# One set of weights a slot, behind the transposes, in an attention and mixture-of-experts kernel, and a new table of step times

## The chip, the cores and the metric

The kernel runs on one core of a Trainium2 chip. The metric is the device time of one execution in microseconds (us). Before the change it is 494.95 us, the median of three runs (494.95 to 495.12).

## What is computed

A causal attention with a memory term, then a layer of eight experts of which each token uses one.

```python
scores = scale * np.matmul(q, k.transpose(0, 1, 3, 2))      # q, k, v: (4, 8, 576, 64)
a = softmax(where(causal, -1e9, scores)); local = a @ v
mem_out = (phi(q) @ M_prev) / (phi(q) . z_prev + 1e-6)
x = g * mem_out + (1 - g) * local                            # 2304 tokens of 512
expert_idx = np.argmax(x @ w_gate, axis=1)                   # 8 experts
for e in range(8):                                           # w1[e]: 512x1024, w2[e]: 1024x512, float32
    xe = x[expert_idx == e]
    out[mask] = gate_w[mask] * (np.maximum(xe @ w1[e], 0) @ w2[e])
```

## The kernel before

**Attention** (`attention`, to about 262 us of the span) is cut into some 545 steps. Each step has a time in units of one pair of heads: a base from the table `K` plus a shift from `K["sh"]`, and the steps are written out sorted by that time, which a scheduler then interleaves further. The table is thus the order of the work on every engine.

**The experts** (`experts`) are written by hand, engine by engine, with semaphores and with branches on the counts that the routing found. Work goes in *slots*: 128 tokens of one expert (a full slot) or 64 (a half one). With these inputs there are 23: expert 0 (in the kernel's own order) has slots 0 to 3, expert 1 slot 4, expert 2 slots 5 to 11, expert 3 slot 12 (half), expert 4 slots 13 to 18 (18 half), expert 5 slot 19 (half), expert 6 slots 20 and 21 (21 half), expert 7 slot 22 (half). Slot 0 is mostly done beside the end of attention. In each slot

- PE multiplies the tokens `xT` by w1 into `ph` (L1632, 96 matmuls), and then the relu of it by w2 into `m_py` (L1648, 24 matmuls; L1645 in half slots). Numbers are kept as a high and a low float16 part.
- DVE makes the two relu parts (L1812, L1814), copies the next slot's transposed tokens to `xT` (L1858), and splits the gathered tokens of the slot after that into `m_xn` (L1835, L1837).
- ACT takes `m_py` out (L1774); POOL gathers tokens for a later slot (L1532) and scatters results (L1547).
- SP issues the two DMA transposes of `m_xn` into `m_xB` (`xtrans`, L1443) and the loads of weights (`load`, L1414).

**Weights** of an expert are eight units of 512 KB, in two *sets* of four: set 0 and 1 are expert 1's, 2 and 3 expert 2's, to 13 for expert 7 (`half_of`). A set is loaded as float32 into one of two stages and converted one set a slot: ACT makes the high part (`conv_hi`, L1302), DVE the low part (`conv_lo`, L1306). In this run sets 0 to 7 are converted in slots 1 to 8, sets 8 to 11 in slots 13 to 16, sets 12 and 13 in slots 19 and 20. Set 0 is loaded during attention.

**SP's queue** in the experts is the place of the change. SP first waits for two gathers and loads set 1. Then each slot has a `turn` or a `rest`: `slot()` issues the transposes of the next slot's tokens as soon as DVE has copied this slot's and made the next `m_xn`, and then come the loads. `ld` counts the sets that were loaded. `turn(i)` belongs to the slot that converts set i, and loads set i+2 in the ordinary case; `rest` belongs to a slot without conversion, and loads each of two sets that is still due. Before L1414 a load waits until the stage that it writes was converted.

```python
for j in (2 * e + 4, 2 * e + 5):          # rest
    if j < 14:
        with SP.If(SP.snap(ld) < j + 1):
            load_next(j)
```

Of the kernel before, what the change touches and what calls it, by code (L numbers as in the profile page):

```python
# [17 lines left out]
K = dict(wa=(6, 0, 2, 0, 0, 1, 1, 1, 1, 1, 2, 0, 3, 0, 1, 1, 1, 1, 0, 0, 1, 0, 0), d=3.668, wt=4, wu=0, wv=0, w3=46, wl1=(17.6, 17.7, 17.9, 18.0), room=48,  # L18
         sz=(2.047, 2.265, 2.085, 2.03), cr=-2.149, cast1=-1.166, tk1=-0.422, phi0=0.086, pt0=1.165, x0=(19.233,
         19.268), e0=(19.944, 21.6), s0=(1.627, 2.769), s1=(0.965, 1.642), p0=(3.152, 2.79), n1=(-0.81, -1.106),  # L20
         n2=(0.194, 0.959), p1=(1.9, 3.343), wd=(8, 8), nc1=0, pact=11, wact=0, pact1=2, wact1=0, nc3=0, cuts=((1,
         2), (0, 0)), rc=7.911, r0=(15.971, 18.056), r1=(19.042, 22.191), ap=(17.127, 17.643), al=(17.821, 18.944),
         at=(19.653, 20.088), k1=-1.476, setup=1.937, v1=2.277, sw=(3.049, 3.089, 3.067, 3.374), sm=(3.763, 3.551,
         3.508), cast=-0.886, castd=0.017, tk=-0.427, tq=-0.544, phi=0.497, pt=2.14, lk=-1.909, lq=-1.882, lv=0.695,
         n=(-0.15, 0.75), s=(1.052, 2.002), p=(2.014, 3.031), m0=(4.286, 4.261), m7=(2.592, 3.428), m=(2.511, 3.7),
         a0=(4.4, 4.852), a=(3.988, 5.201), wl=(14.447, 14.146, 15.631, 16.029, 16.835, 17.187, 17.16, 17.947),
         wc=(15.676, 17.094, 15.773, 17.231, 17.473, 17.338, 18.21, 17.972), sh=dict(m_steps1w=0.45, wconv01=0.43,
         s_steps14w=0.24, a_steps4=1.03, const_q1=3.25, n_first68=0.2, first_q2=0.12, m_steps2w=0.27,
         p_steps2w=-0.01, wload03=-0.03, wconv03=-1.21, s_first12=0.4, setup=-1.59, n_steps4=-0.13, s_steps6w=-0.51,
         p_steps0=0.37, s_steps13=-0.07, phi21=1.15, wload06=1.12, s_steps8w=0.79, wload10=0.62, load6k=-0.45,  # L30
         setup_w0=0.03, n_steps15=-0.7, n_steps13=0.15, n_steps2w=-0.23, load5q=0.2, p_steps12w=0.65,
         bothtrans_piece1=-0.1, load6v=0.06, load2v=-0.16, load4q=0.08, wload13=1.53, wload01=1.01, s_steps12=0.17,
         load1k=-3.84, m_steps7w=-0.93, s_first01=0.72, load_pieceq0=-0.83, n_first56=0.08, p_steps1w=-0.29,
         m_steps5w=0.14, load0v=0.44, n_steps11=-0.23, wload05=-0.16, n_steps12w=-0.49, s_steps3=0.18,
         wconv00=-0.14, a_steps6w=-0.57, p_steps8w=-0.28, n_steps11w=-0.18, cast_q50=-0.25, p_steps9w=-0.37,
         wconv02=-0.38, load5k=-0.19, wconv06=0.84, phi40=0.24, n_first89=0.06, phi60=-0.06, cast_q71=-0.03,
         setup_m2=0.42, cast_k01=0.07, phi50=-0.54, a_steps7=-0.19, cast_q20=-0.12, n_steps7=-0.24, m_steps4=0.95,
         p_steps4=-0.02, p_steps13w=0.12, trans7QT1=0.19, s_first37=0.59, load3k=0.47, m_steps3=0.39,
         s_steps10w=-0.31, wload04=0.19, cast_k10=-0.58, load0k1=0.23, setup_m1=0.24, setup_w3=-0.1, p_steps13=0.3,
         s_steps8=-0.02, setup_w2=0.11, a_steps0w=-0.32, phi70=-0.08, setup_z1=0.65, s_steps9=-0.09, trans0PT=0.42,  # L40
         p_steps14=0.54, p_steps5=0.26, setup_z0=0.25, phi10=-0.14, trans2PT=0.17, p_steps0w=-1.61, cast_k11=0.6,
# [1213 lines left out]
def experts(nc, tc, es, x_dram, mem, rout, w1, w2, out):  # L1255
# [29 lines left out]
    with tc.tile_critical():  # L1285
# [159 lines left out]
        def loads(j):  # L1445

            if j < 14:
                for e, u in half_of(j):
                    if e > 2 and split(e - 2, u) > 0:
                        SP.wait_ge(S["clo"], 16 + split(e - 2, u))  # L1450
                    load(e, u)

        SP.wait_ge(S["g0"], 16)
        SP.wait_ge(S["gg"], 16)
        for u in range(NL, 8):
            load(1, u)
# [3 lines left out]
        SP.reg_mov(ld, 2)  # L1460
# [4 lines left out]
        for e in range(NE):  # L1465
# [16 lines left out]
            def turn(i):  # L1482
                slot()
                if i == c0:
                    SP.wait_ge(S["sc0"], 16)
                    SP.sem_inc(S["ya"], 1)
                SP.reg_add(cr, cr, 1)
                with SP.If(SP.snap(ld) < i + 1):
                    load_next(i)
                with SP.If(SP.snap(ld) < i + 2):  # L1490
                    load_next(i + 1)
                with SP.Else():
                    with SP.If(SP.snap(ld) < i + 3):
                        load_next(i + 2)

            def rest():
                slot()
                for j in (2 * e + 4, 2 * e + 5):
                    if j < 14:
                        with SP.If(SP.snap(ld) < j + 1):  # L1500
                            load_next(j)
# [407 lines left out]
```

## Time and profile before

| | |
|---|---|
| median of three runs | 494.95 us |
| the profiled execution's own time | 495.53 us |
| its span, first to last instruction | 493.8 us |
| PE busy | 458.9 us, 93% |
| DVE, ACT, POOL busy | 355.1, 222.4, 219.5 us |
| attention, about | 0 to 262 us |
| experts, about | 262 to 493.8 us |

How to read it: an engine's busy time counts its own instructions. The chain of waits follows the last instruction back to what released it, again and again. "issue" in it is time in which an engine waited for nothing that the profile shows. The granted clock is 1.00 at TensorE's 2.4 GHz and 0.50 at 1.2 GHz.

### The profile page before, as it was taken

Reading aid. Unit: us, or ns where it says so; the run is one execution under the profiler, and the core shown is the slowest. Engines: PE = TensorE matmul, PEld = TensorE weight load, DVE = VectorE, ACT = ScalarE, POOL = GpSimd, SP = SyncE. Lnnn points to the kernel's source line nnn. Section 1 sums busy time; section 2 is a strip of 40 time slices with the busy share of each in tenths; the row PEclk is TensorE's granted clock in tenths of the full one; section 3 lists DMA queues with packets and bytes.
Section 4 is the critical chain, followed back from the end, with each engine's and each line's share of the span. In section 5 each row is a group of like instructions: output and inputs, shape, how many; then the busy total and the mean of one; then the engine's idle time right before and its main releaser. Section 6 shows DMA issues by size and latency. Waiting matters only on the chain.

```text
span 493.8 us, 14324 instructions
## 1 busy us (share of the span) xinstructions
PE 458.9 (93%) x5274; PEld 311.9 (63%) x5275; DVE 355.1 (72%) x785; ACT 222.4 (45%) x363; POOL 219.5 (44%) x397
## 2 busy tenths in 40 slices
PE   2999889999999989999998899899999998999995
PEld 0654456566566645656675577677667776777865
DVE  3898678687868746889876587788863458874694
ACT  3687665565566556365713324543300033430611
POOL 7467558367748235546542332322232322323332
PEclk9999899999999999999999989999999999999999
DMA  5567979899899979989442999979843393893522
GB/s 119 128 117 167 185 147 174 159 186 217 173 181 166 255 164 178 192 189 288 140 145 76 271 339 300 254 258 284 286 152 90 100 366 83 244 261 100 85 66 73
DMA packets 170184, 90.85 MB, mean 184 GB/s; under 512 B 151487, under 2 KB 152767, under 8 KB 170112
## 3 DMA queue, kind: packets, MB, share of 16 engines
q1 hardware_dynamic: 166192, 77.95, 67.2%
q0 software_dynamic: 3920, 12.10, 7.9%
q8 instruction: 26, 0.43, 0.4%
q14 instruction: 46, 0.38, 0.3%
HBM read 55.64 MB, written 11.60 MB: 136 GB/s over the span
## 4 chain that ended last, share of the span: by engine, by line
PE 61%; SPq 9%; DVE 9%; DMA 8%; issue 7%; ACT 3%; POOL 2%; POOLq 1%; DVEq 0%; ACTq 0%
PE ph L1632 17%; PE m_py L1648 15%; PE o L566 7%; PE st L492 5%; PE sm L597 3%; SPq L276 3%; DMA m_xB<-m_xn 2%; SPq L278 2%; DMA QT<-mem 2%; PE loc L678 2%; PE sn L405 2%; SPq L1443 1%; DVE mem L1306 1%; PE wm L883 1%; DMA mem<-in_q_dram 1%
## 5 line engine op out<-in xcount | busy, mean ns | idle before, releaser
L1632 PE MATMUL ph<-m_xT,mem 128*128 128x128 f16 (+1 forms) x1344 | 68.9, 214 | 5.1 <-DVE m_xT L1858 3.8
L1632 PEld LDWEIGHTS ph<-m_xT,mem 128*128 128x128 f16 x1344 | 67.4, 99 | 8.8 <-issue 6.9
L1812 DVE TENSOR_SCALAR m_hT<-ph 128x512 f16<-128x512 f32 (+1 forms) x44 | 27.7, 630 | 53.2 <-PE ph L1632 43.8
L1774 ACT ACTIVATE m_y<-m_py 128x512 f32<-128x512 f32 x17 | 10.2, 597 | 123.8 <-PE m_py L1648 84.2
L496 POOL TENSOR_SCALAR_AFFINE_SELECT aT<-aT 128x128 f32<-128x128 f32 (+2 forms) x160 | 48.8, 322 | 38.1 <-ACT aT L511 36.0
L511 ACT ACTIVATE aT<-st 128x512 f32<-128x512 f32 x96 | 54.8, 594 | 19.5 <-PE st L492 19.0
L413 DVE TENSOR_REDUCE mt<-sn 128x1 f32<-128x512 f32 (+4 forms) x83 | 54.2, 663 | 13.0 <-PE sn L411 10.4
L1648 PE MATMUL m_py<-mem,m_hT 128*128 128x512 f16 x264 | 58.9, 379 | 0.8 <-DVE m_hT L1812 0.8
L566 PE MATMUL o<-aT,mem 128*64 128x448 f32 (+4 forms) x320 | 57.9, 433 | 0.7 <-POOL aT L496 0.7
L1582 POOL COPY m_ig<-r_idx 128x1 int32 x22 | 12.1, 548 | 96.4 <-DVE m_xn L1835 95.2
L492 PE MATMUL st<-mem 128*128 128x64 f16 (+6 forms) x224 | 46.6, 259 | 0.7 <-ACT aT L511 0.3
L1648 PEld LDWEIGHTS m_py<-mem,m_hT 128*128 128x128 f16 x264 | 25.3, 98 | 29.3 <-DVE mem L1306 0.9
L1632 PE MATMUL ph<-m_xT,m_w 128*128 128x128 f16 (+1 forms) x768 | 42.0, 216 | 1.7 <-issue 1.7
L1632 PEld LDWEIGHTS ph<-m_xT,m_w 128*128 128x128 f16 x768 | 41.1, 98 | 3.8 <-issue 2.1
L492 PEld LDWEIGHTS <-mem 128*128 128x128 f16 (+1 forms) x448 | 32.8, 98 | 16.8 <-issue 5.3
L492 PE MATMUL st<-QT,mem 66*128 66x64 f16 (+6 forms) x224 | 41.7, 259 | 0.0
L1648 PE MATMUL m_py<-m_w,m_hT 128*128 128x512 f16 x168 | 37.4, 379 | 0.0
L1532 POOL DMA_INDIRECT m_xg<-x_scratch,m_ig x23 | 26.3, 1141 | 22.9 <-POOL m_ig L1582 15.8
L566 PEld LDWEIGHTS o<-aT,mem 128*64 128x64 f32 x320 | 22.8, 137 | 18.0 <-issue 11.2
L1547 POOL DMA_INDIRECT out_dram<-m_y,m_is x23 | 24.0, 1042 | 19.6 <-POOL m_is L1553 15.4
L405 PE MATMUL sn<-mem 128*128 128x128 f16 (+3 forms) x158 | 31.4, 276 | 0.5 <-DVE mt L413 0.2
L1814 DVE SCALAR_TENSOR_TENSOR m_hT<-ph,m_hT 128x512 f16<-128x512 f32 (+1 forms) x44 | 27.7, 630 | 1.5
(264 smaller groups left out, 911.0 us busy)
## 6 DMA issues: line engine op xcount, KB each, us to landing
mem<-in_moe_w_dram SPq DMA_DIRECT2D x40, 512.0 KB, 5.0
m_stage<-in_moe_w_dram SPq DMA_DIRECT2D x24, 512.0 KB, 6.9
mem<-in_k_dram SPq DMA_DIRECT2D x32, 128.0 KB, 2.9
mem<-in_q_dram SPq DMA_DIRECT2D x32, 128.0 KB, 3.0
mem<-in_v_dram SPq DMA_DIRECT2D x32, 128.0 KB, 2.8
x_scratch<-xb SPq DMA_DIRECT2D x3, 1152.0 KB, 5.8
mem<-mem SPq DMA_DIRECT2D x6, 288.0 KB, 3.8
x_scratch<-xb SPq DMA_DIRECT2D x1, 864.0 KB, 3.8
```

Source lines behind the costliest of these rows:

```text
L405: nc.tensor.matmul(ps[:, c:c + k1 - k0], QT[:, 5 * hh + t, :], keys(hh)[:, k0:k1], start=(c == 0), stop=(k1 == parts[-1][3] and hh == part ...
L413: nc.vector.reduce_max(out, v, axis=AX.X)
L492: nc.tensor.matmul(ps[:, c:c + n], kk[:, kb, :], qq[:, w:w + n], start=(first and i == 0 and j == 0), stop=(last and i == 1 and j == len(p ...
L496: nc.gpsimd.affine_select(out=ap, in_=ap, pattern=pattern, compare_op=ALU.is_ge, fill=0.0, base=base, channel_multiplier=-1)
L511: nc.scalar.activation(out=a, in_=ps, func=AF.Exp, scale=ESC)
L566: nc.tensor.matmul(o[64 * hh:64 * hh + 64, q0:q0 + n], vv, aa, start=(j == 0), stop=(j == 4), skip_group_check=True)
L1532: G.indirect_dma_start(out=x.rearrange("p h e -> p (h e)"), out_offset=None, in_=x_dram, in_offset=bass.IndirectOffsetOnAxis(ap=i, axis=0) ...
L1547: G.indirect_dma_start(out=out, out_offset=bass.IndirectOffsetOnAxis(ap=i, axis=0), in_=ysb[:, j], in_offset=None, bounds_check=bound, oob ...
L1632: mm = PE.matmul(ph[i2][:, f, 0:N], w[:, kc, c:c + 128], x[:, j, kc, 0:N], start=(i == 0), stop=(i == 11), skip_group_check=True)
L1648: mm = PE.matmul(py, hh, ww[:, 4 + ff // 2, c:c + 512], start=st, stop=sp_)
L1812: V.tensor_scalar(out=hT[i2][0][:, :, 0:N], in0=ph[i2][:, :, 0:N], scalar1=0.0, scalar2=None, op0=ALU.max).then_inc(S[hi], 1)
L1814: V.scalar_tensor_tensor(out=hT[i2][1][:, :, 0:N], in0=ph[i2][:, :, 0:N], scalar=0.0, in1=hT[i2][0][:, :, 0:N], op0=ALU.max, op1=ALU.subtr ...
```

## The change

Two things. The table `K` has other numbers for many of the steps, some of which then stand at another place; two of its lines before and after (`d`: a shift of all the sums of the softmax, `wl1`: the loads of set 0, `p_steps0`: the first product of scores and v):

```diff
-K = dict(wa=(6, 0, 2, 0, 0, 1, 1, 1, 1, 1, 2, 0, 3, 0, 1, 1, 1, 1, 0, 0, 1, 0, 0), d=3.668, wt=4, wu=0, wv=0, w3=46, wl1=(17.6, 17.7, 17.9, 18.0), room=48,
...
-         p_steps0=0.37, s_steps13=-0.07, phi21=1.15, wload06=1.12, s_steps8w=0.79, wload10=0.62, load6k=-0.45,
+K = dict(wa=(6, 0, 2, 0, 0, 1, 1, 1, 1, 1, 2, 0, 3, 0, 1, 1, 1, 1, 0, 0, 1, 0, 0), d=3.629, wt=4, wu=0, wv=0, w3=46,
...
+         s_first12=0.62, setup=-1.73, n_steps4=-0.11, s_steps6w=-0.55, p_steps0=-0.69, s_steps13=-0.07, phi21=0.72,
```

And SP's loads: set 1 is no longer loaded ahead of the first transposes; every turn loads at most one set, the first that is due; the wait for the first scatter (`sc0`) stands behind the loads.

```diff
             if j < 14:
                 for e, u in half_of(j):
+                    if e == 1 and u < NL:
+                        continue
                     if e > 2 and split(e - 2, u) > 0:
                         SP.wait_ge(S["clo"], 16 + split(e - 2, u))
                     load(e, u)
-        SP.wait_ge(S["g0"], 16)
-        SP.wait_ge(S["gg"], 16)
-        for u in range(NL, 8):
-            load(1, u)
...
-        SP.reg_mov(ld, 2)
+        SP.reg_mov(ld, 1 + NL // 8)
...
-            def turn(i):
+            def first_of(js):
+                if js and js[0] < 14:
+                    with SP.If(SP.snap(ld) < js[0] + 1):
+                        load_next(js[0])
+                    with SP.Else():
+                        first_of(js[1:])
+
+            def turn(i, both=False):
                 slot()
+                SP.reg_add(cr, cr, 1 + both)
+                first_of((i, i + 1, i + 2))
+                if both:
+                    first_of((i, i + 1))
                 if i == c0:
                     SP.wait_ge(S["sc0"], 16)
                     SP.sem_inc(S["ya"], 1)
-                SP.reg_add(cr, cr, 1)
-                with SP.If(SP.snap(ld) < i + 1):
-                    load_next(i)
-                with SP.If(SP.snap(ld) < i + 2):
-                    load_next(i + 1)
-                with SP.Else():
-                    with SP.If(SP.snap(ld) < i + 3):
-                        load_next(i + 2)
 
             def rest():
                 slot()
-                for j in (2 * e + 4, 2 * e + 5):
-                    if j < 14:
-                        with SP.If(SP.snap(ld) < j + 1):
-                            load_next(j)
+                first_of(tuple(range(2 * e + 2, 2 * e + 6)))
```

SP's instructions where the experts begin, before (`mem_61` is here the odd experts' stage, so the first DMA row is set 1; `m_stage` is the even experts' stage, `r_cnt` the counts of slots):

```order
L1905 UNCONDITIONAL_BRANCH
L1414 DMA mem_61<-in_moe_w_dram 128x2x512 x4
L1463 TENSOR_LOAD r_cnt
L1464 TENSOR_LOAD r_cnt
L1513 COMPARE_AND_BRANCH
L1515 COMPARE_AND_BRANCH
L1469 ISA
L1516 COMPARE_AND_BRANCH
L1438 ISA
L1443 DMA_TRANSPOSE m_xB<-m_xn_4177 128x4x128
L1442 REGISTER_ALU
L1443 DMA_TRANSPOSE m_xB<-m_xn_4178 128x4x128
```

The same place in the changed program, where load is L1415, the transpose L1444 and the ladder of branches L1483:

```order
L1515 COMPARE_AND_BRANCH
L1439 ISA
L1444 DMA_TRANSPOSE m_xB<-m_xn_4177 128x4x128
L1443 REGISTER_ALU
L1444 DMA_TRANSPOSE m_xB<-m_xn_4178 128x4x128
L1473 TENSOR_LOAD r_cnt
L1475 TENSOR_LOAD r_cnt
L1490 ISA
L1483 COMPARE_AND_BRANCH
L1483 UNCONDITIONAL_BRANCH
L1483 COMPARE_AND_BRANCH
L1415 DMA mem_61<-in_moe_w_dram 128x2x512 x4
```

The four loads of set 1 moved from ahead of the first two transposes to behind them.

SP's instructions in the `rest` of expert 3 (slot 12), before; each load row stands behind a branch of its own:

```order
L1443 DMA_TRANSPOSE m_xB<-m_xn_4178 128x4x128
L1474 TENSOR_LOAD r_cnt
L1476 TENSOR_LOAD r_cnt
L1500 COMPARE_AND_BRANCH
L1414 DMA m_stage_4185<-in_moe_w_dram 128x1024 x4
L1500 UNCONDITIONAL_BRANCH
L1500 COMPARE_AND_BRANCH
L1414 DMA m_stage_4185<-in_moe_w_dram 128x2x512 x4
```

And in the changed program; after each load a jump leads out of the ladder:

```order
L1473 TENSOR_LOAD r_cnt
L1475 TENSOR_LOAD r_cnt
L1483 COMPARE_AND_BRANCH
L1415 DMA mem_61<-in_moe_w_dram 128x1024 x4
L1483 UNCONDITIONAL_BRANCH
L1483 COMPARE_AND_BRANCH
L1415 DMA mem_61<-in_moe_w_dram 128x2x512 x4
L1483 UNCONDITIONAL_BRANCH
L1483 COMPARE_AND_BRANCH
L1415 DMA m_stage_4185<-in_moe_w_dram 128x1024 x4
L1483 UNCONDITIONAL_BRANCH
L1483 COMPARE_AND_BRANCH
```

Before, both sets (10 and 11) go out in this slot; now one of the four choices does, which is set 10, and set 11 is left to a later turn.

In attention, PE at the first product of scores and v (`p_steps0`, `o`), in the changed program:

```order
L884 MATMUL wm<-r_id_66 128x512
L556 MATMUL sl<-aL,mem_61 64x64 x2
L567 MATMUL o<-aT,mem_61 64x512 x2
L567 MATMUL o<-aT,mem_61 64x448 x2
L567 MATMUL o<-aT,mem_61 64x320 x2
L567 MATMUL o<-aT,mem_61 64x192 x2
L567 MATMUL o<-aT,mem_61 64x64 x2
L332 LDWEIGHTS mem_59
```

Before, these ten matmuls stood one or two at a time between transposes and scores of the next heads over some 150 rows; now they are one block ahead of those transposes.

## Rows read from the trace of the kernel before

**Rows 1.** The page: busy us, share of the span and instructions of each engine.

```profile
PE 458.9 (93%) x5274; PEld 311.9 (63%) x5275; DVE 355.1 (72%) x785; ACT 222.4 (45%) x363; POOL 219.5 (44%) x397
```

**Rows 2.** Chain of waits, slots 2 to 4: start us, us, what.

```profile
283.24 7.15 PE ph L1632 x96
290.39 5.18 PE m_py L1648 x24
295.57 5.36 PE ph L1632 x96
...
306.11 5.36 PE ph L1632 x96
```

**Rows 3.** Timeline, slot 1: start us, us, engine, line, what, count, [idle before].

```profile
270.44 0.48 DVE L1835 TENSOR_SCALAR m_xn<-m_xg 128x512 f16<-128x512 f32 x1
270.49 1.93 SPq L1414 DMA_DIRECT2D mem<-in_moe_w_dram  x4
...
274.23 3.19 SPq L1443 DMA_TRANSPOSE m_xB<-m_xn  x2
...
275.92 5.34 PE L1648 MATMUL m_py<-mem,m_hT 128*128 128x512 f16 x24
...
280.73 0.18 POOL L1553 COPY m_is<-r_ids 128x1 int32 x1 [5.66 <-SPq L1486]
...
282.67 0.43 DVE L1858 COPY m_xT<-m_xB 128x1024 f16<-128x1024 f16 x1 [4.00 <-DMA m_xB<-m_xn]
...
283.24 7.15 PE L1632 MATMUL ph<-m_xT,mem 128*128 128x128 f16 x96 [1.98 <-DVE m_xT L1858]
```

**Rows 4.** Windows: us; busy PE, PEld, DVE, ACT, POOL; granted clock; DMA share, GB/s.

```profile
55.00:58.50 3.50, 3.50 (x16) 1.25 (x16) 2.27 (x2) 2.84 (x3) 1.82 (x3) 0.52 0.96 176
...
283.80:287.20 3.40, 3.40 (x36) 3.40 (x34) 2.75 (x3) 2.29 (x3) 1.96 (x3) 0.50 1.02 354
```

**Rows 5.** Chain of waits, slots 12 to 14.

```profile
392.50 0.38 SPq L1414
...
398.42 3.39 SPq L1443
...
401.99 7.35 DMA m_xB<-m_xn
```

**Rows 6.** Timeline, slots 12 to 14.

```profile
397.20 0.75 DVE L1837 SCALAR_TENSOR_TENSOR m_xn<-m_xg,m_xn 128x512 f16<-128x512 f32 x1
...
402.84 5.34 PE L1648 MATMUL m_py<-mem,m_hT 128*128 128x512 f16 x24
...
410.00 4.18 PE L1632 MATMUL ph<-m_xT,mem 128*128 128x128 f16 x72 [1.82 <-DVE m_xT L1858]
```

**Rows 7.** Line 1414, the 52 loads of weights in the experts.

```profile
DMA to landing us min/median/max: 3.4/5.9/9.6
```

**Rows 8.** Timeline, slots 3 and 4: loads, and the next slot's conversion.

```profile
298.56 2.17 SPq L1414 DMA_DIRECT2D mem<-in_moe_w_dram  x4
...
307.97 3.90 ACT L1302 ACTIVATE m_w<-m_stage 128x1024 f16<-128x1024 f32 x4 [1.09 <-issue]
...
310.16 1.22 DVE L1306 SCALAR_TENSOR_TENSOR m_w<-m_stage,m_w 128x1024 f16<-128x1024 f32 x1
...
311.30 5.34 PE L1648 MATMUL m_py<-mem,m_hT 128*128 128x512 f16 x24
...
311.50 0.69 DVE L1812 TENSOR_SCALAR m_hT<-ph 128x512 f16<-128x512 f32 x1
```

**Rows 9.** Timeline, slots 20 and 21: transposes with no load ahead of them.

```profile
476.29 2.56 SPq L1443 DMA_TRANSPOSE m_xB<-m_xn  x2
...
481.87 0.43 DVE L1858 COPY m_xT<-m_xB 128x1024 f16<-128x1024 f16 x1 [1.03 <-DMA m_xB<-m_xn]
```

**Rows 10.** PE's waits in attention (0 to 262 us): us in total, times, longest.

```profile
PE mem L632 <- DMA mem<-mem: 2.6, 2, 2.1
PE st L531 <- DMA QT<-mem: 1.9, 4, 0.8
```

More of the change, by code (lines that the diff above doesn't have):

```diff
@@ new lines @@
+K = dict(wa=(6, 0, 2, 0, 0, 1, 1, 1, 1, 1, 2, 0, 3, 0, 1, 1, 1, 1, 0, 0, 1, 0, 0), d=3.629, wt=4, wu=0, wv=0, w3=46,
+         wl1=(17.749, 17.651, 17.759, 18.218), room=48, sz=(2.047, 2.258, 2.085, 2.03), cr=-2.438, cast1=-1.166,
+         tk1=-0.422, phi0=0.086, pt0=1.4, x0=(19.233, 19.268), e0=(19.954, 21.001), s0=(1.627, 2.769), s1=(0.934,
+         1.642), p0=(3.152, 2.829), n1=(-0.948, -1.042), n2=(0.155, 0.922), p1=(1.978, 3.343), wd=(8, 8), nc1=0,
+         pact=11, wact=0, pact1=2, wact1=0, nc3=0, cuts=((1, 2), (0, 0)), rc=7.839, r0=(15.971, 18.056), r1=(19.042,
+         22.084), ap=(17.237, 17.643), al=(17.821, 19.616), at=(19.771, 20.088), k1=-1.454, setup=1.979, v1=2.357,
+         sw=(3.049, 3.089, 3.067, 3.374), sm=(3.763, 3.551, 3.469), cast=-0.886, castd=0.022, tk=-0.34, tq=-0.561,
+         phi=0.488, pt=2.261, lk=-1.909, lq=-1.889, lv=0.652, n=(-0.15, 0.75), s=(1.049, 2.002), p=(2.014, 3.019),
+         m0=(4.315, 4.261), m7=(2.592, 3.428), m=(2.511, 3.7), a0=(4.376, 4.858), a=(3.988, 5.201), wl=(14.447,
+         14.146, 15.631, 16.029, 16.835, 17.187, 17.16, 17.947), wc=(15.676, 17.037, 15.773, 17.231, 17.473, 17.96,
+         18.205, 18.15), sh=dict(m_steps1w=0.49, wconv01=-0.51, s_steps14w=0.14, a_steps4=1.03, const_q1=3.25,
+         n_first68=0.2, first_q2=0.12, m_steps2w=0.27, p_steps2w=-0.01, wload03=-0.03, wconv03=-1.21,
+         s_first12=0.62, setup=-1.73, n_steps4=-0.11, s_steps6w=-0.55, p_steps0=-0.69, s_steps13=-0.07, phi21=0.72,
+         wload06=1.83, s_steps8w=0.79, wload10=0.88, load6k=-0.45, n_steps15=-0.7, n_steps13=0.13, n_steps2w=-0.23,
+         load5q=0.2, p_steps12w=0.65, bothtrans_piece1=-0.1, load6v=0.06, load2v=-0.16, load4q=0.08, wload13=1.54,
+         wload01=1.01, s_steps12=0.16, load1k=-3.84, m_steps7w=-0.93, s_first01=0.72, load_pieceq0=-0.76,
+         n_first56=0.08, p_steps1w=-0.29, m_steps5w=0.14, load0v=0.44, n_steps11=-0.24, n_steps12w=-0.49,
+         s_steps3=0.18, wconv00=-0.18, a_steps6w=-0.57, p_steps8w=-0.36, n_steps11w=-0.18, cast_q50=-0.25,
+         p_steps9w=-0.39, wconv02=-0.38, load5k=-0.13, wconv06=1.47, phi40=0.24, n_first89=0.06, phi60=-0.06,
+         cast_q71=0.31, setup_m2=0.42, cast_k01=0.15, phi50=-0.54, a_steps7=-0.19, cast_q20=-0.52, n_steps7=-0.24,
+         m_steps4=0.95, p_steps4=-0.02, p_steps13w=0.12, trans7QT1=0.19, s_first37=0.59, load3k=0.47, m_steps3=0.39,
+         s_steps10w=-0.33, wload04=0.75, cast_k10=-0.58, load0k1=0.23, setup_m1=0.24, setup_w3=-0.1, p_steps13=0.22,
+         s_steps8=-0.07, setup_w2=0.11, a_steps0w=-0.32, phi70=0.21, setup_z1=0.59, s_steps9=-0.09, trans0PT=0.42,
+         p_steps14=0.54, p_steps5=0.26, setup_z0=0.33, phi10=-0.14, trans2PT=0.33, p_steps0w=-1.47, cast_k11=0.96,
+         p_steps9=-0.02, cast_q60=0.07, wload17=0.84, n_steps15w=0.38, a_steps3=0.2, p_steps6w=0.69, wconv05=0.66,
+         wconv04=0.27, m_steps7=-0.32, phi01=-0.03, trans4KT1=-0.22, a_steps2=-0.1, a_steps2w=-0.01, m_steps5=-0.02,
+         s_steps12w=-0.89, s_steps14=0.07, p_steps10=0.76, cast_q41=-0.29, trans5QT1=0.18, a_steps7w=-1.04,
+         s_steps7=-0.15, p_steps11w=-0.84, phi41=1.02, s_steps9w=0.16, p_steps8=0.87, bothcast_piece2=0.08,
+         n_steps5w=-0.15, p_steps5w=0.15, s_steps1=0.07, trans7PT=0.13, wconv10=1.48, m_steps4w=-0.84,
+         cast_k50=-0.01, p_steps6=0.12, phi30=-0.42, s_steps4w=0.16, s_steps11=-0.14, m_steps6w=-0.84,
+         n_first1011=0.52, p_steps10w=-0.55, cast_k71=-0.47, n_steps1w=0.4, p_steps7w=0.75, cast_k41=-0.1,
+         p_steps11=0.2, trans3PT=-0.58, d_steps5=-0.52, cast_k30=-0.12, load0q1=-0.61, n_steps10=0.22,
+         load_pieceq1=-0.09, n_steps6w=0.02, trans_pe11=0.41, setup_z3=0.19, d_steps2w=0.41, cast_q11=-0.49,
+         n_steps10w=-0.22, trans4QT1=-0.07, d_steps1=0.18, s_steps10=0.27, n_steps7w=-0.08, cast_k51=-1.06,
+         n_steps9w=-0.32, s_steps5w=-0.04, a_steps4w=0.05, wconv11=-0.74, s_steps5=0.04, d_steps4w=0.92,
+         p_steps15=0.01, routing1=0.4, routing1w=1.2, s_steps3w=-0.16, cast_k61=-0.31, phi20=0.58, s_steps6=0.47,
+         phi71=0.53, s_steps15w=-0.12, warm1=-0.03, bothcast_piece1=-0.09, d_steps0=0.3, setup_w1=0.03,
+         d_steps3=0.25, n_steps6=0.05, m_steps3w=0.09, load2q=-0.14, a_steps3w=0.24, wload11=0.87, cast_q10=-0.49,
+         warm2=1.9, setup_m0=-0.72, d_steps0w=-0.26, wload15=-0.67, routing0=0.05, n_steps5=-0.26,
+         bothcast_piece0=0.04, const_k1=-0.62, phi31=0.29, s_steps11w=0.12, warm3=2.56, cast_k40=-0.79,
+         d_steps7w=-0.42, cast_q31=-0.9, n_steps1=-0.59, wconv07=0.92, d_steps1w=0.17, n_steps9=-0.04, phi00=-0.02,
+         a_tail7w=-0.05, load_pieceq2=0.05, a_pre7w=1.29, wload00=0.6, trans_pe10=0.27, setup_z2=-0.38,
+         const_k0=-0.08, trans5PT=0.05, load_piecek2=0.12, bothtrans_piece0=0.05, n_first25=0.08, cast_q40=0.03,
+         n_steps4w=0.29, load1q=1.54, s_steps15=0.2, d_steps6w=-0.25, s_first23=0.34, d_steps4=-0.99, a_tail7=0.66,
+         trans2QT1=0.01, a_last7w=-1.53, bothtrans_piece2=0.02, n_steps12=0.41, cast_q21=0.16, early_x0=0.66,
+         load3v=-0.02, p_steps14w=0.37, a_pre7=-0.8, const_rest=-0.08, cast_k70=-0.67, a_steps1w=0.03, load7q=0.03,
+         a_last7=0.66, trans7KT1=-0.29, p_steps3w=0.22, d_steps5w=-0.11, trans5KT1=-0.2, a_steps6=0.01,
+         wload02=-0.5, early_x0w=-0.01, trans6KT1=0.23, n_first910=-0.11, cast_q30=-0.28, trans6PT=-0.04,
+         trans2KT1=-0.03, phi61=-0.22, load4k=-0.33, const_k2=-0.57, phi11=0.51, load_piecek1=-0.07, load4v=-0.02,
+         s_steps2=0.34, a_steps5w=0.03, cast_k31=-0.33, first_k2=0.5, cast_k21=0.34, p_steps4w=-0.06, fill46=0.76,
+         n_steps14w=0.02, a_steps1=0.56, trans3KT1=-0.39, cast_k20=0.44, wload07=0.98, p_steps1=0.13, p_steps7=0.04,
+         cast_q51=0.42, early_p0w=0.36, n_steps8w=0.01, s_steps13w=0.05, n_first02=0.03, n_steps14=-0.02,
+         d_steps3w=0.02, m_steps0=-0.11, s_steps4=-0.03, cast_q70=-0.05, n_steps8=0.04, d_steps2=-0.1, consts=-0.03,
+         p_steps15w=0.06, n_steps3w=0.1, trans6QT1=0.06, cast_q01=-0.08, load1v=-0.08, trans3QT1=0.06,
+         early_p0=-0.08))
@@ L1518, in experts @@
                             with SP.Else():
-                                turn(now[0])
-                                SP.reg_add(cr, cr, 1)
+                                turn(now[0], True)
                     with SP.If(SP.snap(cr) < 2 * e + 2):
```

52 lines of the change are left out of this document (removed).

## The prediction

> **What bounds the kernel now.** I read the page first: TensorE is busy for 93% of the span [rows 1], so time can only come from the places where it stands still or runs slowly. Then I went along the chain of waits through the experts, slot by slot. The reader is to see a steady beat there: a full slot is 5.36 us of `ph` and 5.18 us of `m_py`, and the next slot begins 306.11 - 295.57 = 10.54 us after the last [rows 2]. Almost every full slot keeps it. Two do not, and both lead back to SP's queue.
>
> *Stall A, before slot 2.* `m_py` of slot 1 starts at 275.92 [rows 3]. At the steady 5.18 us [rows 2] the next `ph` could start at 281.10; it starts at 283.24 [rows 2], 2.14 us late. The row names DVE's copy of the transposed tokens, which itself waited 4.00 us for the transposes' DMA [rows 3]. SP issued those transposes at 274.23, behind the four loads of set 1 (270.49), though DVE began to make their input at 270.44 [rows 3]. And slot 2's `ph` then takes 7.15 us where slot 3's takes 5.36 [rows 2], because the granted clock is 0.50, the 1.2 GHz level, from 283.8 to 287.2 [rows 4]: 1.79 us more. Stall A with its slow stretch costs 2.14 + 1.79 = 3.93 us.
>
> *Stall B, before slot 14.* `m_py` of slot 13 starts at 402.84 [rows 6], so slot 14 could start at 408.02; it starts at 410.00, 1.98 us late. The chain goes through the transposes' landing (7.35 us), a slow issue of the first one (398.42, 3.39 us) and the eight loads that SP began at 392.50 [rows 5]. These are sets 10 and 11, 4 MB, both from one `rest`.
>
> **The change part by part.**
>
> *Set 1 behind the transposes*. SP's waits for the two gathers vanish, and SP stands ready at `xtrans` when `m_xn` is made. L1835 starts at 270.44 and makes the first half of it in 0.48 us [rows 3], so the pair can go out from about 271.0 instead of 274.23, and takes 2.56 us to issue [rows 9]. With no load ahead, a pair landed 481.87 - 476.29 = 5.6 us after its issue began [rows 9]; from 271.0 that is 276.6. DVE is done with its second conversion of the slot at about 278.7 (its 4.00 us of idle end at 282.67 [rows 3]), copies `xT` in 0.43 us and is done at 279.1, 2 us ahead of 281.10. So stall A goes. Its price is known, 2.14 us; the bounds are nothing (the transposes are late for a reason that I don't see) and 2.14, and I take 2.14, since the pair would have to land over 9 us after its issue to be late again, and with four loads ahead of it, it took 282.67 - 274.23 = 8.4 [rows 3].
>
> *The clock in slot 2.* The slow stretch began half a microsecond after the 1.98 us in which TensorE stood idle [rows 3, 4]. If the idle goes, I expect the clock to stay at 2.4 GHz: 1.79 us more, with the bounds 0 and 1.79. The trace is not all of one mind: the idle of 1.82 us ahead of slot 14 [rows 6] and one of 2.1 us in attention [rows 10] were not followed by a fall, and another slow stretch stands at 55 us [rows 4]. By the Trainium skill, page "TensorE: Matmul & The Clock Gate", section "Part 1: The HAM clock gate", the level follows the engine's recent activity, judged at moments that are not tied to the kernel's own gaps. By that, the sum keeps its 1.79 us only if no other dip is caught at the new times, and would be 1.79 us smaller if one is. The rows alone say so too, and a rival below carries it.
>
> *One set a slot.* In slot 12 SP loads set 10 alone. Its four loads take 2.17 us to issue [rows 8], to about 394.7, so SP is free when the first half of `m_xn` is ready, at 397.20 where L1837 starts [rows 6], and the transposes go out from about 397.3 instead of 398.42 [rows 5], with 2 MB ahead of them instead of 4. Behind one set the pair of slot 1 took 8.4 us from its issue [rows 3], where the loads were issued only 1.8 us ahead; here it is 2.6. 397.3 + 8.4 = 405.7, well ahead of 408.02 less the copy of 0.43. So stall B goes: 1.98 us, bounds 0 and 1.98.
>
> *Later loads.* Sets 1 to 9 are now loaded in slots 1 to 9 instead of 1, 1, 2, ... 8, and set 11 in slot 14 instead of 12. Each is converted at the same place as before, so sets 2 to 7 have one slot between load and conversion instead of two. I cost this at nothing, and the cover is this: a turn's first load goes out at 298.56, and the next slot's first conversion on ACT begins at 307.97 [rows 8], 9.4 us later; the loads land after 5.9 us in the median and 9.6 at most [rows 7], the longest in the burst of eight that goes. The bytes per slot are the same. Set 11 still has two slots, sets 12 and 13 stay where they are, sets 8 and 9 have four or more.
>
> *The wait for `sc0`* goes behind the loads of the first turn. Before, POOL idled 5.66 us until SP passed it at 280.7 [rows 3]. SP now comes to it at about 276.2. If it ends at 280.7 again, SP is held until then; next it must issue slot 3's transposes, whose input is made at about 280 and which are needed shortly ahead of slot 3, at about 289. Nothing.
>
> *More branches on SP*: SP waits for DVE in every slot, so a few branches lie beside that wait. Nothing.
>
> *The table of step times.* It changes the order of attention's steps and not their number. The order shows small moves, `p_steps0` as the largest on TensorE; SP's queue in attention is nearly the same row for row. No row says what a new order costs. The nearest rows are TensorE's waits there: 2.6 us for one kind of transfer, 1.9 for another [rows 10], with the longest of each 2.1 and 0.8. A new order may take such a pair away or make one: -3 to +3 us (2.1 + 0.8 = 2.9). I take 0, as neither sign has a row on its side.
>
> *Sum:* 2.14 + 1.79 + 1.98 = 5.91 us. The profiled execution took 495.53 us by its own time, so 489.62; it was 0.58 us above the median of the runs shown (494.95). Against that median, 494.95 - 5.91 = 489.04, say **489.0 us**.
>
> What is late next: in slots 2 to 17 nothing on the experts' chain but TensorE itself, and the short stop inside slot 5, for which the chain names no releaser.
>
> **The rivals.**
>
> *Late weights (slower).* With one slot of lead, a load that lands too late holds ACT's conversion, DVE's behind it, then the relu of the second half of `ph`, and TensorE. DVE takes the first converted unit at 310.16; ACT needs 3.90 / 4 = 0.98 us for it [rows 8], so the load must land by 309.2, 10.6 us after 298.56. DVE is done with that unit at 311.4 and makes the next relu in 0.69 us; TensorE needs this only after 12 of the 24 matmuls that begin at 311.30 [rows 8], at 313.9, which leaves 1.8 us more. So it decides from a landing at 12.4 us; beyond that, every microsecond counts in each of the seven slots 2 to 8, and slower by over 1 us begins at about 13.4. At 14.4 it costs 7 x 2 = 14 us, and 494.95 - 5.91 + 14 = 503 us. For it: the DMA share is at its limit in these slots (1.02 [rows 4]). Against it: the longest landing is 9.6 [rows 7], and no byte is added. The Trainium skill, page "DMA: Bandwidth & Descriptors", section "Rules for kernel authors", speaks for this rival: a transfer is to be issued early and waited for late. The same page, section "Queues, rings and completion order", speaks for the forecast: what is queued on one ring is taken in its order, as the transposes behind the loads show.
>
> *One of the two stalls stays, or the clock falls elsewhere.* If B stays, 491.0; if the clock falls anyway, 489.04 + 1.79 = 490.8; if stall A stays whole, 493.0.
>
> *Attention loses.* The new order puts `p_steps0`'s ten matmuls ahead of transposes on which SP and ACT wait. A new stop of 3 to 7 us: 492 to 496.
>
> *Attention gains over 3 us*: below 486.
>
> **How the numbers follow.** The forecast, both stalls gone and attention within 3 us: 0.62 (486 to 492). One stall or the clock stays: 0.13 (490.8 to 493.0). Attention loses: 0.14, of which 0.05 is still faster, 0.06 the same, 0.03 slower. Late weights: 0.05, of which 0.01 the same. Attention gains: 0.06. The range 486.0 to 493.0 takes in the first two and some of the third, and leaves out about 0.19. What can be told from no change is 0.2%, about 1.0 us. Faster: 0.62 + 0.13 + 0.06 + 0.05 = 0.86. Same: 0.07. Slower: 0.07.
>
> **What would show it.** Right: the first transposes issued at about 271 in the experts' own time, ahead of all loads; `ph` of slot 2 beginning 10.5 to 10.7 us after that of slot 1 and taking 5.4 us; slot 14 beginning 10.5 us after slot 13; four loads in slot 12. Wrong: DVE or ACT waiting for weights in slots 2 to 8, the copy to `xT` waiting for DMA in slots 2 or 14, a new stretch at 0.50, or the first `ph` of slot 1 later than 273 or earlier than 268, which would be attention's doing.

## The result, and the profile after

The changed kernel takes 488.29 us, the median of four runs (486.79 to 488.69), where the kernel before took 495.03 us beside it (494.95 to 497.74). The ratio is 0.9845, with a 95% interval of 0.9805 to 0.9885. Executions more than 1.5% above the fastest of the same kernel are left out of the medians and ratios in this document. Forecast were 489.0 us and a range of 486.0 to 493.0.

The page of the changed kernel, its span and its first line of busy times (as [rows 1]; the execution's own time is 487.91 us):

```profile
span 486.1 us, 14337 instructions
...
PE 454.6 (94%) x5274; PEld 311.9 (64%) x5275; DVE 356.1 (73%) x785; ACT 222.8 (46%) x363; POOL 218.3 (45%) x397
```

TensorE has the same 5274 matmuls and is busy 4.3 us less; the span is 7.7 us shorter. The chain of waits through the experts (start us, us, what), to hold against [rows 2, 5]:

```profile
270.09 5.52 PE ph L1630 x96
275.61 5.18 PE m_py L1646 x24
280.79 5.36 PE ph L1630 x96
286.15 5.18 PE m_py L1646 x24
291.33 5.36 PE ph L1630 x96
...
312.47 1.56 PE ph L1630 x28
314.03 0.69 issue
314.72 3.96 PE ph L1630 x68
...
392.73 5.47 PE ph L1630 x96
398.19 5.18 PE m_py L1646 x24
403.37 5.36 PE ph L1630 x96
```

From slot 1 to 14 the chain is now TensorE alone, without a copy or a transfer in it, apart from the short stop in slot 5 for which no releaser is named. Slot 2's `ph` takes 5.36 us instead of 7.15, and slot 14 follows slot 13 in 10.55 us.

The timeline of slot 1 (start us, us, engine, line, what, count, [idle before]), as [rows 3]:

```profile
270.13 0.49 DVE L1833 TENSOR_SCALAR m_xn<-m_xg 128x512 f16<-128x512 f32 x1 [0.19 <-DMA m_xg<-x_scratch,m_ig]
...
270.83 2.67 SPq L1444 DMA_TRANSPOSE m_xB<-m_xn  x2
...
274.72 2.21 SPq L1415 DMA_DIRECT2D mem<-in_moe_w_dram  x4
...
277.62 0.62 POOL L1551 COPY m_is<-r_ids 128x1 int32 x1 [3.18 <-SPq L1495]
278.11 0.42 DVE L1856 COPY m_xT<-m_xB 128x1024 f16<-128x1024 f16 x1
```

The transposes go out 0.7 us after DVE begins their input, the loads behind them, and the copy to `xT` has no idle time in front of it: its 4.00 us [rows 3] are gone. The same timeline in slot 12, as [rows 6]:

```profile
388.24 1.99 SPq L1415 DMA_DIRECT2D m_stage<-in_moe_w_dram  x4
...
391.58 0.75 DVE L1835 SCALAR_TENSOR_TENSOR m_xn<-m_xg,m_xn 128x512 f16<-128x512 f32 x1
391.75 12.56 SPq L1444 DMA_TRANSPOSE m_xB<-m_xn  x4
...
400.69 0.42 DVE L1856 COPY m_xT<-m_xB 128x1024 f16<-128x1024 f16 x1
```

Four loads instead of eight, and slot 14's copy waits for nothing (the row counts in the pair that is issued in slot 13, hence its length). The loads of weights (line 1415), as [rows 7]:

```profile
DMA to landing us min/median/max: 4.0/6.0/8.9
```

And windows (us; busy PE, PEld, DVE, ACT, POOL; granted clock; DMA share, GB/s), as [rows 4]:

```profile
182.00:190.00 8.00, 6.96 (x51) 4.32 (x52) 2.72 (x10) 3.67 (x7) 3.95 (x8) 0.57 0.92 184
250.50:254.50 4.00, 4.00 (x15) 2.82 (x16) 3.86 (x15) 0.24 (x1) 1.89 (x3) 0.57 0.36 116
280.00:290.00 10.00, 10.00 (x119) 7.50 (x118) 8.34 (x11) 4.50 (x5) 3.69 (x6) 1.00 1.14 336
```

The slow stretch of slot 2 is gone (1.00 from 280 to 290), and so is the one at 55 us; two others stand in attention, which nonetheless ends 0.47 us earlier (slot 1 begins at 270.09, before at 270.56).

By the times at which TensorE begins a slot, the 7.7 us are: attention 0.47; slot 1 to 2, 2.14; slot 2 to 3, 1.62; slots 4 to 6, 0.52; slot 12 to 13, 0.05; slot 13 to 14, 1.98; slots 18 to 22 and the end, 0.91.

### The profile page after: what moved, and what is told of

Same layout as the page of the kernel before. It is cut to its first block, busy times and chain, and to the rows that moved or that the text cites. A ratio compares the mean times of both kernels' runs of the same rounds, so it can differ in the third digit from the quotient of the medians.

```text
span 486.1 us, 14337 instructions
## 1 busy us (share of the span) xinstructions
PE 454.6 (94%) x5274; PEld 311.9 (64%) x5275; DVE 356.1 (73%) x785; ACT 222.8 (46%) x363; POOL 218.3 (45%) x397
## 4 chain that ended last, share of the span: by engine, by line
PE 70%; DMA 9%; DVE 7%; issue 5%; SPq 3%; ACT 2%; POOL 2%; POOLq 1%; DVEq 0%; ACTq 0%
PE ph L1630 19%; PE m_py L1646 18%; PE o L567 7%; PE st L493 6%; PE sm L598 4%; DMA QT<-mem 3%; PE sn L406 2%; PE loc L679 2%; DMA mem<-mem 1%; DMA mem<-in_moe_w_dram 1%; PE ph L988 1%; DMA mem<-in_k_dram 1%; DMA m_xB<-m_xn 1%; SPq L277 1%; DVE mem L1307 1%
## 5 line engine op out<-in xcount | busy, mean ns | idle before, releaser
L1630 PEld LDWEIGHTS ph<-m_xT,mem 128*128 128x128 f16 x1344 | 65.9, 98 | 4.5 <-issue 2.1
L1630 PE MATMUL ph<-m_xT,mem 128*128 128x128 f16 (+1 forms) x1344 | 67.2, 212 | 1.3 <-DVE m_xT L1829 0.9
L567 PE MATMUL o<-aT,mem 128*64 128x64 f32 (+4 forms) x320 | 54.8, 434 | 1.1 <-POOL aT L497 1.1
```

Of the source, the lines that this page charges most:

```text
L567: nc.tensor.matmul(o[64 * hh:64 * hh + 64, q0:q0 + n], vv, aa, start=(j == 0), stop=(j == 4), skip_group_check=True)
L1630: mm = PE.matmul(ph[i2][:, f, 0:N], w[:, kc, c:c + 128], x[:, j, kc, 0:N], start=(i == 0), stop=(i == 11), skip_group_check=True)
```

## The experiments

Ten further runs were made, of eight other kernels and of these two once more; e7_idle and b2_before are one execution each. Executions of one kernel lie up to some 7 us apart (23 of the kernel before at 492.4 to 499.4 us), and in the profiles attention's end alone moves by 7 us, so each mechanism is read from the slots, which repeat to 0.01 us where nothing waits. The table has, for the profiled execution of each, when slot 1 begins, how long it is from one slot's begin to the next at the places in question, and from slot 1 to slot 22; a full slot without a stop is 10.54 us. Behind it stands the ratio to the kernel before, with its interval.

| kernel | slot 1 at | 1 to 2 | 2 to 3 | 5 to 6 | 13 to 14 | 1 to 22 | ratio |
|---|---|---|---|---|---|---|---|
| before | 270.56 | 12.68 | 12.16 | 11.97 | 12.53 | 212.11 | |
| b2_before | 269.15 | 12.67 | 12.16 | 11.55 | 14.04 | 214.56 | |
| change | 270.09 | 10.54 | 10.54 | 11.39 | 10.55 | 204.91 | 0.9845 |
| a2_change | 272.41 | 10.54 | 10.54 | 10.84 | 10.55 | 205.38 | 0.984 (0.979 to 0.990) |
| e1_queue | 271.33 | 10.54 | 10.54 | 11.67 | 10.55 | 206.70 | 0.988 (0.984 to 0.992) |
| e2_table | 269.25 | 14.34 | 13.38 | 13.03 | 11.87 | 215.08 | 1.003 (0.999 to 1.006) |
| e3_two_sets | 269.51 | 10.54 | 10.54 | 11.11 | 12.97 | 207.64 | 0.992 (0.989 to 0.996) |
| e4_set1_first | 266.72 | 12.81 | 10.54 | 14.39 | 10.55 | 211.13 | 1.002 (0.999 to 1.004) |
| e5_load_mid | 274.05 | 10.54 | 10.54 | 11.91 | 12.24 | 209.41 | 0.996 (0.992 to 1.001) |
| e6_load_late | 273.33 | 10.54 | 10.54 | 12.20 | 10.89 | 221.59 | 1.014 (1.007 to 1.022) |
| e7_idle | 272.34 | 12.95 | 12.16 | 10.89 | 10.55 | 211.33 | |
| e8_cut | 270.82 | 10.54 | 10.54 | 10.84 | 10.55 | 204.73 | 0.982 (0.976 to 0.988) |

**The change in two halves.** e1_queue has SP's new queue with the table `K` of before, e2_table the new table with SP's queue of before:

```diff
 e1_queue:  K as before;  SP's loads as changed
 e2_table:  K as changed; SP's loads as before
```

> SP's new queue with the old table of step times. If the queue carries the whole gain, as in my sum (2.14 + 1.79 + 1.98 us): 495.0 - 5.9 = 489.1 us, slot 2 beginning 10.5 us after slot 1 with a ph of 5.4 us, slot 14 10.5 us after slot 13, and the experts' first slot where it was before (about 270.5). Rival: the shorter instruction stop in slot 5 and the shorter tail (0.6 + 0.7 us, seen with the change but not in my sum) belong to the queue too: 487.8 us. Rival: the clock in slot 2 follows the moment at which attention ends, so that the table has a part in it: ph of slot 2 stays at 7.15 us and the time at 490.9 us.

> The new table with the old SP queue. If the table is worth only the 0.5 us by which the experts begin earlier: 494.5 us, both stalls (2.1 and 2.0 us) still there and ph of slot 2 at 7.1 us. Rival: the shorter tail and stop in slot 5 belong to the table: 493.2 us. Rival: the slow stretch in slot 2 is a matter of when attention ends: ph of slot 2 at 5.4 us and 492.7 us.

e1 has a median of 489.9 us beside 495.5 of before, 5.6 us less (4.0 to 7.8 by the interval of the ratio); e2 has 496.6. In e1 both stalls are gone and slot 2 runs at full clock. In e2 (start us, us, engine, line, what, [wait]) both are back:

```profile
283.59 8.36 PE L1633 MATMUL ph<-m_xT,mem 128*128 128x128 f16 x96 [3.64 <-DVE m_xT L1859]
...
411.96 2.23 PE L1633 MATMUL ph<-m_xT,mem 128*128 128x128 f16 x37 [1.16 <-DVE m_xT L1859]
```

The queue carries the gain. Of e1's two rivals, the one about attention's end falls, since slot 2 runs at full clock with the old table; the shorter tail and the shorter stop did not come with the queue either: slot 19 to 20 takes 6.91 us in e1 (before 6.95, change 6.26), and TensorE stops for 0.51 us in slot 4 and 0.97 in slot 5 (before 1.27 in slot 5, change 0.69). The table alone shows no gain: its interval holds no change, and slot 1 begins at 266.7 to 274.1 us over the nine profiles with the new table (mean 270.9) and at 269.2 to 271.3 over the three with the old (mean 270.3). My 494.5 and 493.2 for e2 were both too low. In its profiled execution slot 2 began 3.80 us late and not 2.1, with 2.84 us of slow clock behind it, and the stop in slot 5 was 2.33, against a stall B of only 1.32.

**Each stall put back alone.** e3_two_sets lets the `rest` of slot 12 load two sets; e4_set1_first loads set 1 ahead of the first transposes:

```diff
 e3:             def rest():
                     slot()
                     first_of(tuple(range(2 * e + 2, 2 * e + 6)))
+                    if e == 3:
+                        first_of(tuple(range(2 * e + 2, 2 * e + 6)))
 e4:
...
+        SP.wait_ge(S["g0"], 16)
+        SP.wait_ge(S["gg"], 16)
+        for u in range(NL, 8):
+            load(1, u)
...
-        SP.reg_mov(ld, 1 + NL // 8)
+        SP.reg_mov(ld, 2)
```

> The changed kernel, but slot 12 loads two sets (10 and 11) as before. If stall B comes from the eight loads ahead of the transposes: slot 14 begins 12.5 us after slot 13 instead of 10.55, and 488.3 + 2.0 = 490.3 us. Rival: it came from the moment of the transposes and not from the second set: 488.3 us.

> The changed kernel, but set 1 is loaded ahead of the first transposes, behind the two gathers, as before. If stall A and the slow clock behind it come from this place alone: slot 2 begins 12.7 us after slot 1, its ph takes 7.15 us, and 488.3 + 3.9 = 492.2 us. Rival: the idle time alone does not make the clock fall: stall A is back, ph stays at 5.4 us, and 490.4 us. Rival: the stall was due to the burst of eight loads (sets 1 and 2 in one slot), not to the order: 488.3 us, or under 489.3.

e3, timeline of slots 12 to 14:

```profile
387.58 5.94 SPq L1415 DMA_DIRECT2D m_stage<-in_moe_w_dram  x8
...
391.26 0.48 DVE L1835 TENSOR_SCALAR m_xn<-m_xg 128x512 f16<-128x512 f32 x1
...
394.88 11.79 SPq L1444 DMA_TRANSPOSE m_xB<-m_xn  x3
...
405.01 2.17 PE L1632 MATMUL ph<-m_xT,mem 128*128 128x128 f16 x36 [2.26 <-DVE m_xT L1858]
```

Eight loads, transposes 3.1 us later than the first half of their input was made (391.74), and TensorE stands still for 2.26 us: stall B is the second set. The median is 490.6 us, as expected. e4, slot 1, and TensorE in slots 2 and 5:

```profile
266.59 0.49 DVE L1835 TENSOR_SCALAR m_xn<-m_xg 128x512 f16<-128x512 f32 x1
266.64 1.93 SPq L1415 DMA_DIRECT2D mem<-in_moe_w_dram  x4
...
270.36 3.45 SPq L1444 DMA_TRANSPOSE m_xB<-m_xn  x2
275.73 1.87 SPq L1415 DMA_DIRECT2D m_stage<-in_moe_w_dram  x4
...
279.53 5.52 PE L1632 MATMUL ph<-m_xT,mem 128*128 128x128 f16 x96 [2.11 <-DVE m_xT L1858]
...
311.48 1.73 PE L1632 MATMUL ph<-m_xT,m_w 128*128 128x128 f16 x28
315.27 5.58 PE L1632 MATMUL ph<-m_xT,m_w 128*128 128x128 f16 x68 [2.06 <-issue]
```

Stall A is back with 2.11 us. In slot 1 SP issues set 1 ahead of the transposes (266.64), the pair at 270.36, and set 2 behind it (275.73), as before the change; the changed kernel has four loads behind the pair too (274.72) and no stall, so the four ahead make it. The pair's first input is made at 267.08; what then holds it is the rest of the loads' issue, and SP's reads of the counts and its branches, which stand behind the loads here and are done by 264.74 in the changed kernel. The two waits for gathers that go back with the loads end at 266.64, ahead of that. The third expectation is not settled: no run has eight loads in slot 1 with the transposes first.

The clock stayed up in slot 2, 5.52 us, as the first rival had it. It fell three slots later, behind the stop in slot 5, where 68 matmuls take 5.58 us and took 3.96 in the changed kernel. The time of the whole does not fit any of the three expectations: the median is 496.2 us, 4 us above the largest, and no less than before although stall B is gone. The profiled execution is the fastest of the twelve (490.65 us, with slot 1 at 266.72), so what the others lost beyond stall A stays open.

**What an idle does to the clock.** e7_idle makes DVE copy `xT` ten times in slots 1 and 6, with the queue as changed; b2_before is the kernel before once more, a2_change the changed one.

```diff
+            if cv and cv[0] in ((1, 0), (3, 4)):
+                for x in range(9):
+                    V.tensor_copy(out=xT, in_=xB).then_inc(S["fx"], 1)
+                    V.wait_ge(S["fx"], 3 + x + 9 * (cv[0] == (3, 4)))
             V.tensor_copy(out=xT, in_=xB).then_inc(S["xc"], 1)
```

> The changed kernel, but DVE copies xT ten times instead of once in slots 1 and 6, so that TensorE stands still for about 2.0 us ahead of slots 2 and 7, with the queue as changed. If an idle of this length is enough for the slow clock behind it: ph of slots 2 and 7 takes 7.15 us instead of 5.36 both times, 3.8 us each in all. Rival: the fall is a matter of chance or of the moment, as the earlier runs suggest (stops of 1.8 to 2.4 us were followed by a fall in some runs and not in others): 5.36 us in at least one of the two. The other slots as in the changed kernel.

> The kernel before, for a second profile. Both stalls again (2.1 and 2.0 us, within 0.5), as they come from the order in SP's queue. If the slow clock in slot 2 belongs to stall A: ph of slot 2 takes 7.15 us again. Rival: it comes and goes: 5.36 us.

> The changed kernel once more, for a second profile beside the others of this study. If the gain sits in the experts and is the same in every execution: slots 1 to 22 take 204.9 us again (212.1 before), within 1 us, and what differs lies in attention and in the instruction stops of slots 4 and 5. Rival: the stalls come and go: 204.9 to 212 us.

TensorE in slots 2 and 7 of e7:

```profile
285.29 7.15 PE L1630 MATMUL ph<-m_xT,mem 128*128 128x128 f16 x96 [2.25 <-DVE m_xT L1860]
...
342.17 5.52 PE L1630 MATMUL ph<-m_xT,m_w 128*128 128x128 f16 x96 [2.04 <-DVE m_xT L1860]
```

The one idle was followed by a slow stretch, the other was not. The second profile of before, in slots 2 and 14:

```profile
281.82 7.15 PE L1632 MATMUL ph<-m_xT,mem 128*128 128x128 f16 x96 [1.98 <-DVE m_xT L1858]
...
409.66 6.92 PE L1632 MATMUL ph<-m_xT,mem 128*128 128x128 f16 x96 [3.33 <-DVE m_xT L1858]
```

Stall A is the same to 0.01 us; stall B was 3.33 us this time and had a slow stretch of its own. Over all profiles, ten stops of TensorE in slots 1 to 18 lasted 1.8 to 2.4 us. Four had a slow stretch behind them (before A and again, e4 slot 5, e7 slot 2: 1.98, 1.98, 2.06, 2.25), six had none (before B, e6, e7 slot 7, e4 A, e3 B, e2 slot 5: 1.82, 1.86, 2.04, 2.11, 2.26, 2.33). All three of 3.3 to 3.6 us had one (b2 B, e6 slot 8, e2 A). And there was no slow stretch in these slots without such a stop. The changed kernel's second profile has none of them again, and 205.38 us from slot 1 to 22, as expected within 1 us.

**Later weights.** e5_load_mid and e6_load_late hold each set back until the slot's first product, or its last relu part, is done:

```diff
             def slot():
                 xtrans()
+                spw("h1", rh)        # e6: "h1lo"
+                SP.reg_add(rh, rh, 1)
```

> The changed kernel, but SP lets each set wait until the first product of the slot (ph) is done, some 3.4 us later than now. If the lead of one slot is long enough, as I costed it at nothing: loads issued at 5.4 us into the slot, landed by 5.4 + 9 = 14.4 us, before the 16 us at which a unit would hold TensorE: no change, 488.3 us. Rival (late weights): DVE or ACT wait for weights in slots 2 to 8, at least 1 us in each: 495 us or more.

> The changed kernel, but SP lets each set wait until the slot's last relu part is made, some 5.6 us later than now (7.6 us into the slot). Landings then come 12 to 17 us after the slot's begin, and the point from which TensorE waits is about 16 us. If that point is right: the idle time of ACT's conversion in front of line 1303 goes to DMA, and TensorE loses 0 to 1 us in a few of the seven slots 2 to 8: 488 to 493 us. Rival: there is more slack than I worked out: 488.3 us and no wait of TensorE. Rival: less slack: over 1 us in every slot, 495 us or more.

e6: who waited for the loads (us in total, times), and TensorE's waits for DVE's copy and the copy's for the transposes, in the experts (us in total, times, longest):

```profile
  ACT mem L1303: 21.0, 20
  ACT m_w L1303: 6.3, 8
```

```profile
PE ph L1634 <- DVE m_xT L1860: 13.1, 7, 3.7
...
DVE m_xT L1860 <- DMA m_xB<-m_xn: 30.4, 12, 5.6
```

ACT waited 27.3 us for weights, 28 times, and TensorE not once for what ACT and DVE make of them. Its seven stops that wait for DVE's copy to `xT` lead on to the transposes. In the median e6 took 506.3 us, as slow as its rival said, and e5 494.1, just short of the 495 of its own, and neither for the rival's reason. e5, timeline of slots 12 to 14, shows the way:

```profile
396.96 0.48 DVE L1837 TENSOR_SCALAR m_xn<-m_xg 128x512 f16<-128x512 f32 x1
...
397.59 1.79 SPq L1415 DMA_DIRECT2D m_stage<-in_moe_w_dram  x4
...
400.73 10.99 SPq L1444 DMA_TRANSPOSE m_xB<-m_xn  x3
...
409.50 0.43 DVE L1860 COPY m_xT<-m_xB 128x1024 f16<-128x1024 f16 x1 [3.54 <-DMA m_xB<-m_xn]
```

Slot 12 begins at 392.01. Its loads now go out 5.6 us into the slot, where the changed kernel has them at 1.3, just ahead of the transposes whose input DVE begins at 396.96: stall A's order again, and TensorE stops for 1.52 us ahead of slot 14. Ahead of slot 6, where it stops for 1.21 us, there is more. Behind slot 3's loads SP stands still for 4.54 us directly behind a branch, with no releaser named (305.20 to 309.74; e6 has 4.48 us at the same branch, the changed kernel 0.12). The next pair, the loads of slot 4 and the pair behind them come late after it; that last pair goes out at 318.96, 2.1 us into slot 5 instead of 1.5 us ahead of it. The two runs thus change more than the moment of the weights; what they show is that weights somewhat later cost nothing here by themselves: in e6 ACT begins a slot's first unit by up to 0.8 us later than in the changed kernel (2.92 against 2.11 us into slot 5) and its last by up to 4.6 (8.64 against 4.01 in slot 7). The Trainium skill, page "DMA: Bandwidth & Descriptors", section "Rules for kernel authors", has it that a transfer is issued early and waited for late. The runs agree with it for the transposes; for the weights they show no price of the slot of lead that the change gives up.

**A version that goes further.** In slot 20 of the changed kernel four conversions on DVE stand ahead of its first relu, and TensorE waits 0.80 us for it; in slot 19 DVE waits 1.79 us for transposes. e8_cut puts one conversion there.

```diff
-         pact=11, wact=0, pact1=2, wact1=0, nc3=0, cuts=((1, 2), (0, 0)), ...
+         pact=11, wact=0, pact1=2, wact1=0, nc3=0, cuts=((1, 2), (0, 1)), ...
```

> The changed kernel, but in half slots DVE makes the low part of one unit of weights ahead of the copy to xT instead of behind it; this only concerns slot 19. In the changed kernel DVE waits 1.79 us there for the transposes, and in slot 20 the four conversions hold the first relu and TensorE 0.80 us. If one conversion fits into that wait: slot 20 to 21 takes 10.6 to 10.7 us instead of 11.50, 0.8 us less in all, 487.5. Rival: the unit is not yet made by ACT when DVE comes to it, or the copy is late by it: slot 19 to 20 longer by up to 1.2 us, and 488.3 to 488.7.

```profile
456.09 1.22 DVE L1307 SCALAR_TENSOR_TENSOR mem<-mem,mem 128x1024 f16<-128x1024 f32 x1
...
458.68 5.52 PE L1630 MATMUL ph<-m_xT,mem 128*128 128x128 f16 x96 [0.54 <-DVE m_xT L1856]
...
464.04 5.34 PE L1646 MATMUL m_py<-mem,m_hT 128*128 128x512 f16 x24
```

The conversion at 456.09 lies in DVE's wait, the wait of `m_py` in slot 20 is gone, and slot 20 to 21 takes 10.54 us instead of 11.50, 0.96 less. But slot 19 to 20 takes 7.07 us, where the changed kernel's two profiles have 6.26 and 6.84, and slots 18 to 22 together take 29.70 us against 29.64 and 30.34. The median is 489.14 us where the changed kernel had 489.73 beside it. So the gain is shown in slot 20, and not for the whole.

## Why the prediction was right

*Stall A* (2.14 us): right, to the size. The transposes were forecast for about 271.0 and went out at 270.83, the copy was forecast to be free of its wait and is. e4 brings 2.27 us back (12.81 against 10.54) by putting these four loads ahead again.

*The clock in slot 2* (1.79 us): gone as forecast, but mis-sized by 0.17 us. I took 7.15 - 5.36 from the chain, where a `ph` that follows `m_py` without a gap is counted 0.16 us short, from the end of the product in front; from start to start the slow slot cost 12.16 - 10.54 = 1.62 us. The reason I gave held only half. That the clock stays up where nothing stops, every profile shows for these slots. That a stop of 2 us costs a slow stretch was true in four of ten. The rows of one execution could not give that share, although I had an idle without a fall in hand [rows 6]. The Trainium skill, page "TensorE: Matmul & The Clock Gate", section "Part 1: The HAM clock gate", has it that the level is judged at moments that are not tied to the kernel; the runs are in keeping with it, with a stop of 2.25 us followed by a fall and one of 2.33 not.

*Stall B* (1.98 us): right, 12.53 - 10.55 = 1.98, and e3 brings 2.42 back with the second set. In b2_before the same stall cost 3.49 us and 1.40 behind it, so the profile I had summed up was a mild one.

*Later loads*, *the wait for `sc0`*, *more branches*: nothing, right. The longest landing is 8.9 us, under the 9.6 of before; ACT's conversions in slots 2 to 8 wait for no DMA; POOL comes past its wait at 277.62, earlier than before. The late-weights rival would decide where a slot's first unit is 1.8 us and more later than DVE needs it; even e6 did not bring the first unit that far, so its point of decision was not reached and is not tested, while the changed kernel is well short of it. What I set down for that rival, that the DMA share of 1.02 was at its limit, was misread: from 280 to 290 us it is 1.14 in the changed kernel.

*The table* (0, within 3 us): right as far as the runs can tell. e2's ratio is 1.003 with no change in its interval, and attention's end moves by 7 us among executions of the same table.

*The sum.* My terms were 5.91 us and measured 2.14 + 1.62 + 1.98 = 5.74 in the profile of the change. The other 1.95 us of 7.7 were not in it: 0.47 in attention, 0.52 in the stops of slots 4 to 6, 0.05 behind slot 12 and 0.91 behind slot 18. None of them is shown to be a steady gain: slot 19 to 20 takes 6.84 us in the second profile of the change (6.26 in the first, 6.95 before), and slot 5 to 6 varies from 10.84 to 11.67 under the new queue. The queue alone (e1) gave 5.6 us in the median, close to the sum; with an interval of 4.0 to 7.8 us, so close a fit is luck. The two stalls put back one at a time do not add up to the whole either: e3 and the changed kernel differ by about what was expected, and e4 by more than both stalls together.

Two chances were badly set. "The clock falls elsewhere" got a share of 0.13 with another case, and the clock did fall elsewhere, in attention (182 and 251 us), though the experts began no later for it. A new stretch at 0.50 stood among my signs of being wrong, and it was none. And "attention loses" was priced as a matter of the new order, where the runs show no effect of the order beside a spread of 7 us between executions.

## What to carry to other kernels

Where one queue issues both a small transfer that the next step needs and bulk that a later step needs, put the small one first and give the bulk out in steps: that was 5.6 of 495 us here (e1), with no byte and no instruction fewer. A wait put in such a queue to delay the bulk can delay the small transfer behind it as well (e5, e6). And when a stop of TensorE is priced from one profile, price the slow clock behind it as a chance, and look at a second profile for the stop's own size.

## What was not expected of the hardware

The stop in slot 5, for which no releaser is named, differs from profile to profile. Where set 1 goes out ahead of the transposes it was 1.27 us (before), 0.85 (b2), 2.33 (e2) and 2.06 (e4); behind them it was 0.69 (change), 0.97 (e1), 0.41 (e3), 0.19 (e7), and none in e5 and e6. A part of the gain in slots 4 to 6 may thus belong to the queue, which no run tests. Where it shows, the stop comes after 28 or 30 of the 96 matmuls of another expert's first slot, and SP's long stops in e5 and e6 come directly behind a branch. The profile counts packets of instructions among the DMA queues (74 in the whole changed kernel). The Trainium skill, page "Runtime: NRT & Kernel Launch", section "Instruction fetch mechanics", says that a jump out of the instructions at hand makes the engine fetch them by DMA before it goes on. That would fit a stop that is longer where more loads are in flight, but no run here tests it, and the cause stays open.

Also open is what moves attention's end by 7 us between executions. The slow stretches in it differ from profile to profile (near 55, 61, 185 or 250 us, in e2, e7 and b2 also at 10), but they do not account for it: the kernel before begins slot 1 at 270.56 with 3.4 us of them in attention, and its second profile at 269.15 with 17.1 us.
